# Attention and a two-layer network in one kernel: the first q, k, v transfers in another order and size, and two stores issued at the join

## The chip, the cores and the metric

One Trainium2 chip, one of its cores. The metric is the device time of one execution in microseconds (us), smaller is better; runs of one kernel are given by their median. The profiled execution is a further one, with a time of its own.

## The reference

Softmax attention over 8 batches, 12 heads, 448 positions and 64 columns per head, then a two-layer network over the 3584 tokens, without biases and with a leaky ReLU between the layers:

```python
scores = scale * np.matmul(q, k.transpose(0, 1, 3, 2))
attn = np.exp(scores - np.max(scores, axis=-1, keepdims=True))
attn = attn / (np.sum(attn, axis=-1, keepdims=True) + 1e-09)
x = np.matmul(attn, v).transpose(0, 2, 1, 3).reshape(3584, 768)
h = x @ w_in                       # 768 x 2048
out = np.maximum(0.01 * h, h) @ w_out   # 2048 x 768
```

All arrays are float32 in DRAM; the kernel computes in bfloat16 with float32 sums.

## The kernel before

**Units.** Attention is cut into 48 units: a unit is two heads of one batch, six units to a batch. For each unit the kernel loads q, k and v (`in_q`, `in_k`, `in_v`), brings them as bf16 into the layouts it needs (`cast`, into `qkb` for q and k, into `v_old`, shown as `x_mix`, for v), turns q and k so that the 64 columns lie on partitions (`transposes`, on TensorE in this part, L301, copied out by VectorE, L305), multiplies q and k (`scores`, L319, four chunks of keys, each into one of three PSUM slots `sc`), takes the exponential on ScalarE (`expo`, L331 and L334), multiplies with v (`pv` and `pairs`, L362, with a column of ones in v that gives the sums), and divides on VectorE (L374, L375). Results `x` are turned into `xT`, on TensorE (L389) or by a DMA transpose on SyncE's queue (L276).

**Network.** Seven blocks of tokens (`cuts`) go through both layers as soon as their units are done; block 0's first layer (L424) is woven between the units of the second batch, later blocks between those that follow. Both layers use sums and differences of blocks of the matrices and of the data (`mix_*`, `deep*`), which saves products. The rest of attention is placed between the second layer's products (`second`, `place`).

**Who does what at the start.** The order of all instructions is written by hand: each engine runs its own in the order in which the program emits them, and waits on semaphores. SyncE's queue loads k and q of unit 0 and k of unit 1 as float32 (`load_one`, L173). GpSimd (POOL) issues all other loads (`load_soft`, L163; `load_w`, L215); these convert to bf16 on the way. Such transfers go through one queue, one behind the other. There are eight semaphores for them, given out in turn: a transfer that gets one again waits until the former one has landed. POOL's issue of a load and POOL's casts share POOL's one instruction stream.

`load_soft(u, n, which)` loads n consecutive units in one transfer per array. `room` gives the tile to load into: at first pieces of tiles that are needed later (`w_in_mix`, `w_mix`, `o`, `deep_mix`, `c`), then tiles of a pool (`fq`, `fk`, `fv`). A tile has room for two units. L219 to L230 issue the loads of the start: q of unit 1; q and then k of units 2 and 3; v of unit 0; v of 1 and 2; q and k of 4 and 5; v of 3 and 4; v of 5; the first piece of w_in (columns 0 to 511).

**The first batch.** `first(u)` runs for u = 0 to 5 and emits: scores of chunks 0 and 1 (and 2, for u below 2) and their exponentials, the transposes of x of unit u - 2, the transposes of q and k of unit u + 1 (eight products), `pv` of unit u - 1 in two halves, and scores and exponentials of the other chunks. The casts of units 0, 1 and 2 and that of v of unit 0 are VectorE's (with ScalarE for unit 0), in `first(0)` and ahead of it; from unit 3, and v of unit 1, on they are POOL's. `supply(u)` emits POOL's part of each step from a list: casts of q and k of a unit (`qk`), of v (`v`), loads, pieces of the weights (`w`).

**Stores.** In the second layer `block_pair(i, c)` computes two row tiles `o1` and `o2` of block i. `late` finishes `o1` with a `join` (VectorE, L698) and appends its store to the list `put`; `put_out` issues what is on the list (`store`, L402, on SyncE's queue). It is called by `late` itself only in the last block; else by `second` after 16 steps of the next pair or at the end, and by `place` after rows of x. SyncE's queue works in order: a DMA transpose or a store that waits holds what is behind it. The tiles `o` come from a pool of three.

Of the kernel before, what the change touches and what calls it, by code (L numbers as in the profile page):

```python
# [10 lines left out]
BF16 = mybir.dt.bfloat16  # L11
# [5 lines left out]
def kernel(  # L17
# [24 lines left out]
    NR = len(cuts) - 1  # L42
# [76 lines left out]
    h = h_pool.tile([P, MD, (KEEP + 1) * P], BF16, name="h")  # L119
# [10 lines left out]
    raw = {}  # L130
# [4 lines left out]
    for t in (w_in_mix, w_mix):  # L135
        t = t.rearrange("p x k n -> p (x k n)")
# [9 lines left out]
    def room(x, new):  # L146

        n = P if x and new else SC
        if not rooms:
            return ld_pool.tile([n, 2, NSC, D], F32, name="f" + "qkv"[x])  # L150
        return rooms.pop(0)[:n].bitcast(F32).rearrange("p (h so d) -> p h so d", h=2, so=NSC)

    def load_soft(u, n, which):
        b, hp = divmod(u, HP)
        hs = slice(2 * hp, 2 * hp + 2 * n)
        for x in which:
            new = x > 0 and u >= HY
            t = room(x, new).rearrange("p h so d -> p (h so d)").bitcast(BF16)
            t = t.rearrange("p (u h so d) -> p u h so d", u=2, h=2, so=NSC)
            for p, so, keys in ((slice(0, D), NSC, slice(0, NSC * D)), (slice(D, P), KC, slice(NSC * D, S))) if new else (  # L160
                (slice(0, SC), NSC, slice(0, S)),
            ):
                nc.gpsimd.dma_start(  # L163
                    out=t[p, :n, :, :so].rearrange("p u h so d -> p (u h) (so d)"),
                    in_=(q, k, v)[x][b, hs, keys].rearrange("h (p so) d -> p h (so d)", so=so),
                )
            for i in range(n):
                raw.setdefault(u + i, {})[x] = t[:, i]

    def load_one(u, x, queue):  # L170
        b, hp = divmod(u, HP)
# [7 lines left out]
    def load(u, parts=(0, 1, 2)):  # L179
        if u < NU and u % 2 == 0:  # L180
            load_soft(u, 2, parts)

    def cast(u, parts=(0, 1, 2), by=nc.gpsimd.tensor_copy):
        if u >= NU:
            return
        for x in parts:
            f = raw[u].pop(x)
            t = qkb[u % NB]
            if x < 2 and (x == 0 or u < HY):
                by(t[:SC, x].rearrange("p so h d -> p h so d"), f)  # L190
            elif x == 1:
                if u < HY + NB:
                    nc.gpsimd.memset(t[:, 1, KC], 0.0)
                by(t[:, 1, :KC].rearrange("p so h d -> p h so d"), f[:, :, :KC])
                by(t[:D, 1, KC, 0], f[:D, 0, KC])
                by(t[D:, 1, KC, 1], f[:D, 1, KC])
            elif u < HY:
                by(v_old[:, u % NV, :, :, :D], f)
            else:
                t = v_sb[u % NV]  # L200
                by(t[:, :2 * KC, :D].rearrange("p (h so) d -> p h so d", h=2), f[:, :, :KC])  # L201
                by(t[:D, 2 * KC, :D], f[:D, 0, KC])
                by(t[D:, 2 * KC + 1, :D], f[:D, 1, KC])
# [7 lines left out]
    def load_w(n=1):  # L211
        for _ in range(n):
            if w_steps:
                o, i = w_steps.pop(0)
                nc.gpsimd.dma_start(out=o, in_=i)  # L215
# [3 lines left out]
    load_one(1, 1, nc.sync)  # L219
    ident = const_pool.tile([P, P], BF16)  # L220
    make_identity(nc, ident)
    load_soft(1, 1, (0,))
    load_soft(2, 2, (0, 1))
    load_soft(0, 1, (2,))
    load_soft(1, 2, (2,))
    load_soft(4, 2, (0, 1))
    load_soft(3, 2, (2,))
    load_soft(5, 1, (2,))
    load_w(1)

    warm = h_mix.rearrange("p m c t -> p (m c t)")[:, :512]
    nc.vector.memset(warm, 0.0)
# [160 lines left out]
    def store(o, t0, cols=slice(0, DM), queues=(nc.sync, nc.sync)):  # L393

        queues = list(queues)
        done = 0
        while done < P:
            b, j = divmod(t0 + done, S)
            so, p = divmod(j, SC)
            n = min(SC - p, P - done)  # L400
            dst = out[b * S:(b + 1) * S].rearrange("(p so) n -> so p n", so=NSC)
            queues.pop(0).dma_start(out=dst[so, p:p + n, cols], in_=o[done:done + n, cols])  # L402
            done += n
# [104 lines left out]
    def token(i, x):  # L508

        return KEEP * P if x == KEEP else cuts[i] + x * P  # L510
# [98 lines left out]
    kept, parts, put = {}, [], []  # L609

    def put_out():

        while put:
            store(*put.pop())
# [50 lines left out]
    def block_pair(i, c):  # L665
# [17 lines left out]
        def product(ps, x, w, first=False, cols=slice(0, NW)):  # L683
            for m in range(MH):
                if m in (2, 4, 6):
                    yield
                nc.tensor.matmul(  # L687
                    ps[:, cols], x[:, m], w[:, m], start=(first and m == 0), stop=(m == MH - 1), skip_group_check=True,
                )

        def keep(o, at, ps, by=nc.vector.tensor_copy):
            by(o[:, at], ps[:, :NW])  # L692
# [4 lines left out]
        def join(o, at, ps):  # L697
            nc.vector.tensor_add(o[:, at], o[:, at], ps[:, :NW])  # L698
# [22 lines left out]
        def late():  # L721
            yield from product(b, s3, t3)
            if i:
                keep(o2, left, b, calm)
            join(o2, right, b)
            if i + 1 == NR:
                store(o2, t0, right)
            yield
            yield from product(a, h[:, hi, one], w_out_sb[:, hi, right])
            join(o1, right, a)  # L730
            put.append((o1, token(i, x1)))
            if i + 1 == NR:
                put_out()

        def closing():
# [42 lines left out]
        for x, _ in enumerate(late()):  # L778
            if i and not c and (x == 4 or x == 6 and i + 1 == NR):
                next(parts[0])  # L780
            yield
# [75 lines left out]

    def supply(u):

        for what, n, *parts in {0: [('qk', 3), ('v', 1), ('v', 2), ('load', 6)], 1: [('qk', 4), ('v', 3), ('load', 8, (0, 1))], 2: [('qk', 5), ('v', 4), ('w', 1)], 3: [('qk', 6), ('v', 5), ('w', 1)], 4: [('qk', 7), ('v', 6), ('load', 10, (0, 1)), ('load', 8, (2,))], 5: [('qk', 8), ('v', 7), ('load', 10, (2,)), ('load', 12)]}[u]:  # L860
            if what == "qk":
                cast(n, (0, 1))
            elif what == "v":
                cast(n, (2,))
            elif what == "load":
                load(n, *parts)
            else:
                load_w(n)

    def first(u):  # L870
# [23 lines left out]
        if u + 1 < HP:  # L894
            supply(u)
# [4 lines left out]
        if u + 1 == HP:  # L900
            supply(u)
# [354 lines left out]
```

## Time and profile before

| | |
|---|---|
| time, median of 3 runs | 378.96 us (378.73 to 379.22) |
| profiled execution: time | 379.29 us |
| profiled execution: span of the instructions | 377.5 us |
| granted TensorE clock, mean | 0.995 of full speed |
| VectorE, ScalarE, GpSimd busy | 255.2, 259.8, 193.6 us |
| DMA: bytes moved | 48.08 MB, 127 GB/s over the span, 189 in the first 30 us |
| TensorE busy in the first 30 us | 26.3 us |
| TensorE busy from 30 to 110 us | 79.9 us |

How to read it: times count from the start of the span. PE is TensorE, DVE VectorE, ACT ScalarE, POOL GpSimd; SPq is SyncE's queue of DMA issues. A row of a group or time line names the engine, the line of the kernel, the operation, the tile written and the tile read, and how many instructions were merged (x6). In square brackets stands the idle time of the engine just before, and what ended it; that is inferred, and where the engine named had long been done it was another, mostly a DMA. Granted clock is TensorE's, as a share of full speed.

### The profile page before, as it was taken

To read this page: it belongs to the slowest core of one execution; us is meant where nothing else is said; L and a number is where in the kernel's file an instruction comes from. 1 tells how busy PE (TensorE), PEld (TensorE's weight loads), DVE (VectorE), ACT (ScalarE), POOL (GpSimd) and SP (SyncE) were. 2 spreads that over 40 slices of the span, in tenths; PEclk is the share of its full clock that TensorE was granted. 3 is DMA by queue.
4 is the path that set the end of the run, shared out by engine and by line. 5 is a ranking of instruction groups with operands and counts; after the bars stand their busy time and mean duration, and the time that the engine had idled before them with its cause. 6 is when DMAs were issued, how large, how long until landed. Compare 5 with 4: busy or idle time off the path is not lost.

```text
span 377.5 us, 10113 instructions
## 1 busy us (share of the span) xinstructions
PE 370.0 (98%) x4008; PEld 265.7 (70%) x4008; DVE 255.2 (68%) x558; ACT 259.8 (69%) x399; POOL 193.6 (51%) x376
## 2 busy tenths in 40 slices
PE   7999999999999999999999999999999999999996
PEld 3665657755698556996569966599665995679765
DVE  5666758778666867666687675775747775675763
ACT  6897885866768876658766587666787668526721
POOL 8985972985168889624388234792338020000000
PEclk9899999999999999999999999999999999999999
DMA  9999999998499977974869748889445740131123
GB/s 160 200 204 206 194 198 201 143 153 170 72 185 103 170 119 120 202 159 62 130 139 143 157 64 79 175 136 178 63 65 108 132 109 0 38 98 42 44 63 106
DMA packets 99600, 48.08 MB, mean 127 GB/s; under 512 B 64608, under 2 KB 96352, under 8 KB 99552
## 3 DMA queue, kind: packets, MB, share of 16 engines
q0 software_dynamic: 39600, 22.47, 44.8%
q1 hardware_dynamic: 59504, 24.50, 33.0%
q8 instruction: 31, 0.51, 0.6%
q10 hardware_dynamic: 448, 0.47, 0.4%
q14 instruction: 17, 0.14, 0.1%
HBM read 45.61 MB, written 11.01 MB: 150 GB/s over the span
## 4 chain that ended last, share of the span: by engine, by line
PE 94%; DMA 2%; DVE 1%; issue 1%; ACT 1%; SPq 0%; POOL 0%; DVEq 0%; POOLq 0%; ACTq 0%
PE g L687 29%; PE g L548 14%; PE sc L548 14%; PE sc L322 7%; PE sc L350 6%; PE sc L319 4%; PE g L424 4%; PE sc L650 4%; PE sc L362 3%; PE g L824 2%; PE sc L343 2%; PE g L362 1%; PE g L301 1%; DMA w_in_mix<-in_q_dram 1%; DMA out_dram<-o 1%; PE sc L424 1%
## 5 line engine op out<-in xcount | busy, mean ns | idle before, releaser
L331 ACT ACTIVATE e<-sc 128x896 bf16<-128x896 f32 (+1 forms) x144 | 123.6, 922 | 30.6 <-PE sc L322 20.5
L687 PE MATMUL g<-w_out_sb,h 128*128 128x384 bf16 (+1 forms) x440 | 84.1, 325 | 0.2 <-DVE o L692 0.2
L687 PEld LDWEIGHTS <-h 128*128 128x128 bf16 x592 | 54.4, 98 | 41.8 <-issue 11.7
L537 ACT ACTIVATE h<-c 128x512 bf16<-128x512 f32 (+1 forms) x72 | 43.1, 610 | 30.2 <-DVE c L563 12.4
L548 PEld LDWEIGHTS <-w_in_sb 128*128 128x128 bf16 x576 | 54.6, 98 | 5.7
L190 POOL COPY qkb<-fq 112x512 bf16<-112x512 bf16 x34 | 25.2, 741 | 46.0 <-DMA qkT<-qkb 37.0
L548 PEld LDWEIGHTS <-w_in_mix 128*128 128x128 bf16 x432 | 40.5, 98 | 3.7
L201 POOL COPY v<-fv 128x384 bf16<-128x384 bf16 x30 | 18.6, 618 | 41.5 <-PE sc L350 36.3
L692 DVE COPY o<-g 128x384 f32<-128x384 f32 x47 | 25.9, 552 | 14.7 <-PE g L687 11.4
L350 PE MATMUL sc<-v,e 128*128 128x65 bf16 x720 | 33.3, 193 | 0.0
L981 DVE RECIPROCAL rec<-sc 112x8 f32<-112x8 f32 x42 | 8.7, 207 | 35.8 <-PE sc L350 16.6
L322 PE MATMUL sc<-qkT 64*128 64x448 bf16 (+1 forms) x210 | 32.8, 352 | 0.0
L350 PEld LDWEIGHTS <-e 128*128 128x128 bf16 x720 | 31.2, 98 | 1.3
L982 DVE TENSOR_TENSOR x<-sc,rec 112x512 bf16<-112x512 f32 x42 | 29.0, 691 | 1.6 <-DVE rec L981 0.2
L548 PE MATMUL g<-xT,w_in_sb 128*128 128x256 bf16 (+1 forms) x216 | 28.5, 268 | 0.0
L548 PE MATMUL sc<-xT,w_in_sb 128*128 128x256 bf16 (+1 forms) x216 | 28.5, 268 | 0.0
L698 DVE TENSOR_TENSOR o<-o,g 128x384 f32<-128x384 f32 x39 | 21.3, 549 | 8.7 <-PE g L687 3.9
L343 PE MATMUL sc<-v,e 128*128 128x130 bf16 x120 | 26.5, 221 | 0.0
L654 DVE TENSOR_TENSOR o<-o,sc 128x192 f32<-128x192 f32 x39 | 13.7, 351 | 18.3 <-PE sc L650 18.3
L687 PE MATMUL g<-w_mix,h 128*128 128x384 bf16 x128 | 24.6, 326 | 0.0
L163 POOL DMA_DIRECT2D fv<-in_v_dram x32 | 20.2, 648 | 4.9 <-DMA fq<-in_q_dram 1.5
L362 PEld LDWEIGHTS <-e 112*128 112x128 bf16 x432 | 20.8, 100 | 2.1 <-issue 0.8
(149 smaller groups left out, 744.4 us busy)
## 6 DMA issues: line engine op xcount, KB each, us to landing
fq<-in_q_dram POOLq DMA_DIRECT2D x17, 224.0 KB, 6.1
w_out_sb<-in_moe_w_out_dram POOLq DMA_DIRECT2D x4, 768.0 KB, 12.6
out_dram<-o SPq DMA_DIRECT2D x7, 336.0 KB, 3.4
w_in_sb<-in_moe_w_in_dram POOLq DMA_DIRECT2D x2, 1152.0 KB, 12.6
out_dram<-o SPq DMA_DIRECT2D x7, 288.0 KB, 3.9
fk<-in_k_dram POOLq DMA_DIRECT2D x15, 128.0 KB, 6.1
fv<-in_v_dram POOLq DMA_DIRECT2D x15, 128.0 KB, 5.3
out_dram<-o SPq DMA_DIRECT2D x7, 240.0 KB, 3.3
```

The lines of the kernel that those rows point to most:

```text
L190: by(t[:SC, x].rearrange("p so h d -> p h so d"), f)
L322: nc.tensor.matmul(ps[:, j, :S].rearrange("p (so s) -> p so s", so=NSC), t[p, 1, c], t[p, 0, :, :SC], start=True, stop=True,)
L331: nc.scalar.activation(e[:, :, c, :], ps[:n, :, :S], AX.Exp, scale=scale)
L343: nc.tensor.matmul(ps, e[:, EM + qc * SC:EM + qc * SC + P], vt[:, 2 * KC:].rearrange("p j d -> p (j d)"), start=True, stop=False, skip_gro ...
L350: nc.tensor.matmul(ps[:, j * (D + 1):(j + 1) * (D + 1)], e[:, at:at + P], vt[:, j * KC + c], start=False, stop=(c == KC - 1), skip_group_c ...
L362: nc.tensor.matmul(ps[:, qc, :], t[:SC, at:at + P], vt[:, c], start=(c == 0), stop=(c == NSC - 1),)
L537: nc.scalar.activation(hs[:, m:m + 2, cols], x.rearrange("p (m t) -> p m t", m=2), AX.Prelu, alpha=0.01)
L548: nc.tensor.matmul(ps[:, j * nh:(j + 1) * nh], w[:, kk, ts(j, P)], x[:, kk], start=(first and j == 0 and kk == 0), stop=(kk == KH - 1), sk ...
L687: nc.tensor.matmul(ps[:, cols], x[:, m], w[:, m], start=(first and m == 0), stop=(m == MH - 1), skip_group_check=True,)
L692: by(o[:, at], ps[:, :NW])
L698: nc.vector.tensor_add(o[:, at], o[:, at], ps[:, :NW])
L982: nc.vector.tensor_mul(x, ps[:, :, :, :D], rec.to_broadcast([SC, 2, 2 * NP, D]))
```

## The change

Three things are changed.

1. The loads at the start. `load_soft` can be given a tile and a place in it, so that two transfers share a tile. q and k of units 2 and 3, one transfer each before, become four transfers of one unit, and the order becomes: q of 1, q of 2, k of 2, v of 0, q of 3, k of 3, then v of 1 and 2 and the rest as before. q of 1 and 2 share a tile, as do k of 2 and 3. POOL issues two loads more; bytes and sizes of the packets are the same.
2. The first piece of w_in is no longer issued at the end of the start's loads, but in `supply(0)`: behind POOL's casts of q and k of unit 3 and of v of unit 1, ahead of that of v of unit 2. The list for `supply` changes in this entry alone.
3. `late` calls `put_out` at the join in block 0 and in the last two blocks, where before it did in the last block alone. On SyncE's queue `o1`'s store of the first pair then stands ahead of one DMA transpose of x, once in block 0 and once in block 5; in block 0 two stores at the end of the second pair change places.

The instructions of TensorE, VectorE and ScalarE stay the same, in the same order.

```diff
-    def load_soft(u, n, which):
+    def load_soft(u, n, which, into=None, at=0):
...
-            t = room(x, new).rearrange("p h so d -> p (h so d)").bitcast(BF16)
+            t = (room(x, new) if into is None else into).rearrange("p h so d -> p (h so d)").bitcast(BF16)
...
-                    out=t[p, :n, :, :so].rearrange("p u h so d -> p (u h) (so d)"),
+                    out=t[p, at:at + n, :, :so].rearrange("p u h so d -> p (u h) (so d)"),
...
-                raw.setdefault(u + i, {})[x] = t[:, i]
+                raw.setdefault(u + i, {})[x] = t[:, at + i]
...
-    load_soft(1, 1, (0,))
-    load_soft(2, 2, (0, 1))
+    shared = [room(x, False) for x in (0, 1)]
+    load_soft(1, 1, (0,), shared[0])
+    load_soft(2, 1, (0,), shared[0], 1)
+    load_soft(2, 1, (1,), shared[1])
     load_soft(0, 1, (2,))
+    load_soft(3, 1, (0,))
+    load_soft(3, 1, (1,), shared[1], 1)
     load_soft(1, 2, (2,))
     load_soft(4, 2, (0, 1))
     load_soft(3, 2, (2,))
     load_soft(5, 1, (2,))
-    load_w(1)
...
             put.append((o1, token(i, x1)))
-            if i + 1 == NR:
+            if not 0 < i < NR - 2:
                 put_out()
...
-        for what, n, *parts in {0: [('qk', 3), ('v', 1), ('v', 2), ('load', 6)],
+        for what, n, *parts in {0: [('qk', 3), ('v', 1), ('w', 1), ('v', 2), ('load', 6)],
...
```

More of the change, by code (lines that the diff above doesn't have):

```diff
@@ L858, in supply @@
     def supply(u):
-        for what, n, *parts in {0: [('qk', 3), ('v', 1), ('v', 2), ('load', 6)], 1: [('qk', 4), ('v', 3), ('load', 8, (0, 1))], 2: [('qk', 5), ('v', 4), ('w', 1)], 3: [('qk', 6), ('v', 5), ('w', 1)], 4: [('qk', 7), ('v', 6), ('load', 10, (0, 1)), ('load', 8, (2,))], 5: [('qk', 8), ('v', 7), ('load', 10, (2,)), ('load', 12)]}[u]:
+        for what, n, *parts in {0: [('qk', 3), ('v', 1), ('w', 1), ('v', 2), ('load', 6)], 1: [('qk', 4), ('v', 3), ('load', 8, (0, 1))], 2: [('qk', 5), ('v', 4), ('w', 1)], 3: [('qk', 6), ('v', 5), ('w', 1)], 4: [('qk', 7), ('v', 6), ('load', 10, (0, 1)), ('load', 8, (2,))], 5: [('qk', 8), ('v', 7), ('load', 10, (2,)), ('load', 12)]}[u]:
             if what == "qk":
```

## The prediction

> **What bounds the kernel now.** I read the shares first, then who TensorE (PE) waits for, then the time lines of the stretch in which it waits, engine by engine.
>
> ```profile
> PE 370.0 (98%) x4008; PEld 265.7 (70%) x4008; DVE 255.2 (68%) x558; ACT 259.8 (69%) x399; POOL 193.6 (51%) x376
> ```
>
> PE is busy 370.0 of 377.5 us. An edit that leaves its instructions alone (this one leaves PE's, DVE's and ACT's order as it is) has 7.5 us of idle time and slow clock to work on. Who PE waits for from 23 us to the end:
>
> ```profile
> PE g L687 <- DVE o L692: 0.2, 1, 0.2
> PE sc L319 <- ACT e L331: 0.2, 1, 0.2
> ```
>
> So behind 23 us PE waits 0.4 us in all; what else there is lies in the start and behind its last product (374 us). PE, then ACT, there (start, length, engine, line, idle time before and its releaser):
>
> ```profile
> 8.80 1.05 PE L319 MATMUL sc<-qkT 64*128 64x448 bf16 x6 [0.42 <-DVE qkT L305]
> 9.78 0.37 PE L301 MATMUL g<-ident,qkb 112*128 112x112 bf16 x4
> 10.60 0.52 PE L301 MATMUL g<-ident,qkb 112*128 112x112 bf16 x4 [0.45 <-DVE qkb L190]
> ```
>
> ```profile
> 9.30 2.55 ACT L331 ACTIVATE e<-sc 112x896 bf16<-112x896 f32 x3
> 12.52 0.92 ACT L334 ACTIVATE c<-sc 112x896 bf16<-112x896 f32 x1 [0.67 <-PE sc L319]
> 14.00 2.53 ACT L331 ACTIVATE e<-sc 112x896 bf16<-112x896 f32 x3 [0.56 <-PE sc L319]
> ```
>
> Unit 2's eight transposes are cut in half: the four of q run, the four of k wait 0.45 us for VectorE's cast. Behind them stand P·V of unit 0, the last scores of unit 1 and the first of unit 2, and ACT's exponentials of those start 0.67 + 0.56 = 1.23 us late. After 14.00 ACT shows no idle time until 27.2, and PE is paced by it until 23.05; from there PE runs through. What ACT gains before 14.00 the end gains. Why the cast is late, DVE and then POOL:
>
> ```profile
> 7.02 0.29 DVE L190 COPY qkb<-w_in_mix 112x512 bf16<-112x512 bf16 x1 [1.39 <-DMA w_in_mix<-in_q_dram]
> 8.66 0.65 DVE L190 COPY qkb<-w_in_mix 112x512 bf16<-112x512 bf16 x1
> 9.32 1.22 DVE L190 COPY qkb<-w_in_mix 112x512 bf16<-112x512 bf16 x1
> 10.46 0.28 DVE L198 COPY x_mix<-w_in_mix 112x512 bf16<-112x512 bf16 x1
> ```
>
> ```profile
> 8.38 0.85 POOL L215 DMA_DIRECT2D w_in_sb<-in_moe_w_in_dram  x1 [0.42 <-PE sc L319]
> 9.21 1.17 POOL L190 COPY qkb<-w_in_mix 112x512 bf16<-112x512 bf16 x2
> 11.06 1.17 POOL L198 COPY x_mix<-w_in_mix 112x512 bf16<-112x512 bf16 x2 [0.68 <-DMA w_in_mix<-in_v_dram]
> ```
>
> One copy takes 0.29 us at 7.02, 0.65 us under w_in's issue, and 1.22 us under POOL's two casts of unit 3: it ends 0.16 us behind them (10.54 against 10.38), so it stood still meanwhile. POOL's casts kept their 0.62 us each. Both the late landing of k (below) and this collision come from units 2 and 3 sharing a transfer.
>
> Lastly the granted clock, by 3.4 us windows (PE's busy time is the second number, the clock stands behind POOL's):
>
> ```profile
> 3.85:7.26 3.41, 2.63 (x27) 1.37 (x25) 1.02 (x5) 2.21 (x5) 3.35 (x5) 1.00 1.19 180
> 7.26:10.67 3.41, 2.30 (x22) 1.11 (x23) 2.94 (x6) 3.41 (x5) 2.68 (x4) 1.00 1.42 191
> 10.68:14.08 3.40, 3.40 (x42) 2.29 (x42) 1.83 (x6) 2.17 (x4) 3.02 (x5) 0.50 1.44 196
> ```
>
> PE was busy 2.30 us in the second window, and the third ran at half clock; behind 2.63 us it did not.
>
> **The change, part by part.**
>
> *Transfers.* DMA issues, with KB and us to landing:
>
> ```profile
> w_in_mix<-in_k_dram POOLq DMA_DIRECT2D x1, 224.0 KB, 6.3
> w_in_mix<-in_v_dram POOLq DMA_DIRECT2D x1, 224.0 KB, 6.6
> w_in_mix<-in_q_dram POOLq DMA_DIRECT2D x1, 112.0 KB, 5.5
> w_in_mix<-in_v_dram POOLq DMA_DIRECT2D x1, 112.0 KB, 6.2
> ```
>
> With POOL's issue times these landed thus: q of unit 1 at 1.53 + 5.5 = 7.0; k of 2 and 3 at 3.0 + 6.3 = 9.3; v of 0 at 3.7 + 6.2 = 9.9; v of 1 and 2 at 4.4 + 6.6 = 11.0. POOL's next instruction after q of 2 and 3 waited for their landing: 8.38. From 7.0 to 11.0 these are 784 KB in 4.0 us, about 0.58 us for each 112 KB, and the small v transfer took the same 0.58 as half a large one: splitting costs the queue nothing that shows. So after the change, by bytes ahead in the queue (estimates): q2 7.7, k2 8.4, v0 8.9, q3 9.3, k3 9.9, v of 1 and 2 as before.
>
> *VectorE.* Its copy of unit 1's transposes still ends at 8.74. Then q2, k2 and v0 are all there and POOL has no cast to run before q3's landing at 9.3: three copies of 0.29 us end near 9.6. Upper bound: each meets POOL as at 9.32, and v0 ends at 10.7 as now. I take the free row, since POOL's cast is the only thing that has shown the long one and comes after them.
>
> *PE.* No cut in the transposes: eight from 9.78 in 0.41 us (the later groups of eight are followed 0.41 us on), P·V of unit 0 starts at 10.2 instead of 10.91. It then lasts 0.5 us (the pace of P·V at 14.41) instead of 1.0. With the half clock still granted from 10.68: scores of chunk 3 end at 11.2, the second half of P·V at 12.2, unit 2's first scores at 12.75; the exponential at 14.00 starts at 12.8, a gain of 1.2. With full clock all that is ready by 11.9, and ACT's own chain sets 14.00 − 1.23 = 12.77. Either way about **1.2 us**; bounds 0 (upper bound above) and 1.4 (ACT's lengths overlap by up to 0.1 us an instruction).
>
> By the clock rows the second window gains 0.45 us of transposes and P·V, 2.75 us or more, above the 2.63 that kept the clock. The Trainium skill, "TensorE: Matmul & The Clock Gate", Part 1, has these 4096-cycle windows free-running, not reset when a kernel starts; the 3.41 us agree with the trace. By that rule the same idle time may fall into other windows in other executions, which would move the sum between 1.0 and 1.4; no run here shows another phase.
>
> *POOL.* Two more issues of 0.70 us. Its order: v5's issue to 9.2, casts q3 and k3 to 10.5 (k3 lands at 9.9), v1's cast at 11.06 as now, then w_in's issue to 12.5, v2's cast to 13.1, unit 6's three issues to 15.2. So POOL is 0.9 us later than before. Who waits behind it: unit 4's casts (end 16.3; PE wants them at 18.63 − 1.2 = 17.4), v2 (13.1 against 16.3), unit 5 (19.4 against 20.6). It catches up at 21.84, where it stood waiting for a landing anyway. Cost 0; without this cover 0.9.
>
> *w_in.* Issued at 11.7 instead of 8.38. The queue in front of it holds the same bytes: in the packet records the data of v5 end at 14.2 and w_in's follow at once, although it was issued 5.7 us before; an issue takes some 2.2 us to its first packet (1.53 to 3.70). 11.7 + 2.2 = 13.9: no gap, at worst 0.3 us. PE uses w_in at 25.89, its data end at 17.8. Cost 0.
>
> *Stores.* The diff also puts blocks 0 and 5's stores at the join:
>
> ```profile
> 333.14 0.56 DVE L692 COPY o<-g 128x384 f32<-128x384 f32 x1 [1.17 <-DMA out_dram<-o]
> 329.63 1.04 SPq L402 DMA_DIRECT2D out_dram<-o  x2
> ```
>
> DVE waits 1.17 us for a buffer whose store was queued on SP behind a transpose that had to wait until 328.4; its join was done at 324.6. Stored there it lands some 4 us sooner, and PE's 0.21 us at 333.75 go. On SP two issues of 0.5 us now stand ahead of that transpose, which has 3 us of room, and in block 0 ahead of one at 88.49, which may slip 0.5 us; PE waits for neither. Gain **0.2**, bounds 0 and 0.2.
>
> *Sum.* 1.2 + 0.2 = 1.4: span 377.5 → 376.1. The profiled execution took 379.29, 0.33 above the median of 378.96; from the median, 377.6.
>
> **Rivals.** About 0.2% (0.76 us) is what a measurement of this kernel can tell from no change: "faster" is below 378.2.
>
> B, *the collision moves on to v0.* k2 is early, but v5's issue delays q2 as w_in's did (0.65), q3's cast gets in at 9.3, and VectorE's k2 or v0 stands until k3's cast ends near 10.5. P·V starts at 10.7: gain 0.2, with the stores 378.5. For: DVE at 9.32 did not get in between two casts. Against: k3 lands only at 9.9, which leaves gaps. The Trainium skill, "SBUF — State Buffer", "Who interferes with whom", says the same as a rule: a VectorE copy in a two-port mode and a GpSimd instruction lock each other out for a whole instruction, and the first to start wins. By that rule B decides at 9.3; the 1.22 us agree with it.
>
> C, *VectorE loses to POOL's whole row of casts (slower).* Place: the same port, one copy earlier. If v5's issue holds q2 to 9.3 and q3's cast starts ahead of k2, k2 stands to 10.5 and ends at 10.8; v0 then ends at 11.1 only if it starts before v1's cast at 11.06, or else behind it (0.6 us) near 11.95. P·V of unit 0 then starts at 12.0 instead of 10.91: 378.96 + 1.1 − 0.2 = 379.8. It decides at the end of q2's copy: later than 9.3, or q3 landed before it. For: w_in's issue did hold q2 by 0.36 us at 8.66. Against: the 0.29 us copy at 7.02 met v5's and v3's issues and was not held, and k3's landing leaves POOL a gap.
>
> D, *it runs into landings that do not move.* The queue is saturated to 85 us, so a PE that is 1.2 us earlier meets data at their old times. The closest is unit 6's k: cast at 22.4, wanted at 24.98 − 1.2 = 23.8. If 1.3 us of lateness on the queue ate that, only the stores' gain is left: 378.75.
>
> E, *the clock gate closes one window later.* PE, early, waits for ACT's buffers between 10.68 and 14.09; if it is busy there for less than some 2.3 to 2.6 us, 14.09 to 17.5 runs at half clock. That window holds 3.2 us of PE work at full clock and loses 1.6: 378.96 − 1.4 + 1.6 = 379.2. Against: I count about 3.0 us of work there.
>
> **How the numbers follow.** Forecast 0.62 (377.2 to 378.1: from 1.4 early with 0.2 of spread between runs, to 0.65 early where one of the three copies is held for a cast), B 0.18, D 0.07, C 0.06, E 0.04, something not seen 0.03. Faster: the forecast and mild forms of B and D, 0.67. Slower: C and what is not seen, 0.09. Same: the rest, 0.24. The range reaches from ACT's full overlap with some 0.3 of spread between runs, 376.9, over B and D to 378.9.
>
> **What would show it.** Right: PE's 0.45 us before L301 near 10.6 gone, three VectorE copies of about 0.3 us before 9.7, ACT's third group of exponentials at 12.8, no DVE wait for out at 333. Wrong: a copy of 1 us on VectorE at 9.3 to 10.5 (B), the k2 copy itself late (C), clock 0.50 behind 14.1 (E), or PE's early gain gone again between 17 and 60 us (D).

## The result and the profile after

| | before | after |
|---|---|---|
| time, median of 22 runs each, on the same chip | 378.70 us (377.88 to 379.22) | 379.62 us (378.28 to 381.49) |
| after over before, 95% interval | | 1.0027 (1.0015 to 1.0039) |
| profiled execution: time and span | 379.29, 377.5 us | 381.49, 379.7 us |
| granted clock, mean | 0.995 | 0.999 |

After is slower by 0.9 us, where 1.4 us of gain were forecast. Its profiled execution is the slowest of its 22: its stalls are read for their place, and prices come from the medians.

The early part went as forecast. Time lines of after, VectorE, then TensorE, then ScalarE (start, length, engine, line, operation; the diff moves all lines behind L222 on by three):

```profile
8.69 0.49 DVE L190 COPY qkb<-w_in_mix 112x512 bf16<-112x512 bf16 x2
9.09 0.41 DVE L198 COPY x_mix<-w_in_mix 112x512 bf16<-112x512 bf16 x1
```

```profile
10.62 0.57 PE L304 MATMUL g<-ident,qkb 112*128 112x112 bf16 x8
```

```profile
6.93 2.53 ACT L334 ACTIVATE e<-sc 112x896 bf16<-112x896 f32 x3 [1.19 <-PE sc L322]
9.34 0.93 ACT L337 ACTIVATE c<-sc 112x896 bf16<-112x896 f32 x1
10.14 2.55 ACT L334 ACTIVATE e<-sc 112x896 bf16<-112x896 f32 x3
12.53 0.97 ACT L337 ACTIVATE c<-sc 112x896 bf16<-112x896 f32 x1
13.32 2.59 ACT L334 ACTIVATE e<-sc 112x896 bf16<-112x896 f32 x3
```

The three copies end at 9.50, the eight transposes of unit 2 run uncut, and ScalarE has no idle time from 6.93 to 26.57. Its third group starts 6.39 us behind its first; in the profile of before it was 7.91 us. Yet it starts at 13.32, not at 12.8, for the first group is 0.8 us later than before: 0.68 us are left of the gain in this profile (14.00 to 13.32). The windows of 3.4 us (TensorE's busy time second, granted clock behind the five busy times, last GB/s of all transfers) show no half clock in after:

```profile
7.26:10.67 3.41, 2.22 (x20) 0.93 (x19) 1.77 (x6) 3.41 (x5) 3.20 (x5) 1.00 1.30 167
10.68:14.08 3.40, 3.15 (x67) 2.49 (x66) 2.03 (x6) 3.40 (x5) 2.50 (x5) 1.00 1.40 186
14.09:17.50 3.41, 3.20 (x60) 2.19 (x57) 2.30 (x8) 3.41 (x6) 3.41 (x7) 1.00 1.17 171
```

The last number is the first sign of trouble: 171 GB/s from 14.09 to 17.50, where before moved 208. TensorE's waits in after (us in total, times, longest) name what is new behind 23 us:

```profile
PE sc L322 <- DMA qkT<-qkb: 1.4, 1, 1.4
...
PE g L690 <- DVE o L701: 0.6, 1, 0.6
PE sc L322 <- DVE x L985: 0.5, 1, 0.5
```

**The queue.** POOL's time line in after:

```profile
9.53 1.16 POOL L190 COPY qkb<-w_in_mix 112x512 bf16<-112x512 bf16 x2 [0.15 <-ACT e L334]
11.59 0.61 POOL L198 COPY x_mix<-w_in_mix 112x512 bf16<-112x512 bf16 x1 [0.90 <-DMA w_in_mix<-in_v_dram]
12.14 0.85 POOL L215 DMA_DIRECT2D w_in_sb<-in_moe_w_in_dram  x1
```

The issue of w_in stands behind v of unit 1's cast, which waited for its landing until 11.59. So it starts at 12.14. The first packet of w_in follows at 14.64, 2.5 us after the start of the issue; the data of v of unit 5, ahead of it, had ended at 14.55. From 14 to 24 us the DMA view gives GB/s in 40 slices of 0.25 us, before and then after:

```profile
GB/s 193 223 205 215 197 262 193 205 197 209 193 201 205 201 207 188 197 197 186 197 197 199 197 191 195 199 199 195 193 197 197 199 195 191 201 195 197 213 201 215
DMA packets 3146, 2.01 MB, mean 201 GB/s; under 512 B 101, under 2 KB 3145, under 8 KB 3145
```

```profile
GB/s 174 217 117 129 139 164 180 180 180 184 168 184 197 180 188 180 176 193 166 172 176 119 135 156 162 180 178 164 180 174 186 197 197 199 191 197 193 197 201 195
DMA packets 2731, 1.76 MB, mean 176 GB/s; under 512 B 89, under 2 KB 2730, under 8 KB 2730
```

After drops to 117 GB/s at 14.5 and again to 119 at 19.25, and only from 21.5 on it stays above 185. In ten us it moves 1.76 MB instead of 2.01; at 201 GB/s that is 1.2 us of transfers lost. The ends of the data in the queue, from counting the bytes of its packets:

```
us, end of data         before   after   later by
v of unit 5              14.01   14.55    0.54
w_in, first piece        17.91   19.14    1.23
q, k, v of 6 and 7       21.43   23.07    1.64
w_in, last piece         35.17   36.84    1.67
w_out, first piece       48.14   51.35    3.21
q, k of 14 and 15        63.49   66.96    3.47
```

The step to 3.2 us is POOL's: its first issue of w_out stands behind a cast that waits for a landing, and moves from 41.12 to 43.33. POOL in after:

```profile
41.89 1.50 POOL L198 COPY x_mix<-o 112x512 bf16<-112x512 bf16 x2 [0.45 <-DMA o<-in_v_dram]
43.33 0.75 POOL L215 DMA_DIRECT2D w_out_sb<-in_moe_w_out_dram  x1
```

**Where TensorE pays.** At 41 us. VectorE's time line of before, then of after:

```profile
36.44 0.56 DVE L473 TENSOR_TENSOR w_in_mix<-w_in_sb 128x768 bf16<-128x768 bf16 x1 [1.89 <-DMA w_in_sb<-in_moe_w_in_dram]
```

```profile
38.33 0.56 DVE L476 TENSOR_TENSOR w_in_mix<-w_in_sb 128x768 bf16<-128x768 bf16 x1 [3.29 <-DMA w_in_sb<-in_moe_w_in_dram]
38.92 1.15 DVE L476 TENSOR_TENSOR w_in_mix<-w_in_sb,w_in_mix 128x768 bf16<-128x768 bf16 x2
39.99 0.20 DVE L984 RECIPROCAL rec<-sc 112x8 f32<-112x8 f32 x1
40.23 0.69 DVE L985 TENSOR_TENSOR x<-sc,rec 112x512 bf16<-112x512 f32 x1
```

The sums over w_in's last piece start 1.9 us later; the division of a unit stands behind them in VectorE's order and frees the PSUM slot of the next scores only at 40.92. TensorE, after:

```profile
39.90 0.55 PE L322 MATMUL sc<-qkT 64*128 64x448 bf16 x4
40.97 0.36 PE L322 MATMUL sc<-qkT 64*128 64x448 bf16 x2 [0.52 <-DVE x L985]
```

The next unit's scores follow at 44.50, 4.60 us behind 39.90; before had 3.91 (40.54 to 44.45). In this profile that costs 0.69, which uses up the 0.68 us of lead. At 73 us, TensorE and POOL of after:

```profile
73.59 0.55 PE L322 MATMUL sc<-qkT 64*128 64x448 bf16 x4
75.54 0.36 PE L322 MATMUL sc<-qkT 64*128 64x448 bf16 x2 [1.39 <-DMA qkT<-qkb]
```

```profile
67.47 0.88 POOL L190 COPY qkb<-fq 112x512 bf16<-112x512 bf16 x1 [8.87 <-DMA fq<-in_q_dram]
```

Unit 14's cast (63.52 before) and with it its turning by DMA are 4 us late, and the last two products wait. What follows is 1.62 us later than before (the second layer's products resume at 75.83 against 74.21). The third wait, 0.56 at 88.47, isn't the change's alone: a further profile of before shows 0.56 at 85.73. So the 0.68 us that were left of the early gain were spent at 41 us, and the wait at 75 us made after slower.

### The profile page after: what moved, and what is told of

Same layout as the page of the kernel before. It is cut to its first block, busy times and chain, and to the rows that moved or that the text cites. A ratio compares the mean times of both kernels' runs of the same rounds, so it can differ in the third digit from the quotient of the medians.

```text
span 379.7 us, 10119 instructions
## 1 busy us (share of the span) xinstructions
PE 370.2 (97%) x4008; PEld 265.9 (70%) x4008; DVE 257.2 (68%) x558; ACT 259.8 (68%) x399; POOL 192.0 (51%) x378
## 4 chain that ended last, share of the span: by engine, by line
PE 91%; ACT 3%; DMA 2%; DVE 1%; issue 1%; POOL 0%; ACTq 0%; DVEq 0%; POOLq 0%
PE g L690 29%; PE g L551 14%; PE sc L551 14%; PE sc L325 7%; PE sc L353 6%; PE g L427 4%; PE sc L653 4%; PE sc L322 3%; PE sc L365 3%; ACT e L334 3%; PE sc L346 2%; DMA qkT<-qkb 2%; PE g L827 1%; PE g L304 1%; DMA w_in_mix<-in_k_dram 1%; PE g L365 1%
## 5 line engine op out<-in xcount | busy, mean ns | idle before, releaser
L690 PEld LDWEIGHTS <-h 128*128 128x128 bf16 x592 | 54.4, 98 | 41.8 <-issue 11.7
L190 POOL COPY qkb<-fq 112x512 bf16<-112x512 bf16 x34 | 23.9, 704 | 46.7 <-DMA qkT<-qkb 36.8
L322 PE MATMUL sc<-qkT 64*128 64x448 bf16 x144 | 20.1, 355 | 3.7 <-DMA qkT<-qkb 1.4
```

The costliest lines, as they stand in the source:

```text
L322: nc.tensor.matmul(ps[:, j, :S], t[p, S + c * SC:S + c * SC + P], t[p, :S], start=True, stop=True)
L690: nc.tensor.matmul(ps[:, cols], x[:, m], w[:, m], start=(first and m == 0), stop=(m == MH - 1), skip_group_check=True,)
```

## The experiments

Three things were open: what each part is worth by itself; whether the early gain is real; and how a w_in that TensorE first needs at 25.9 us can cost anything. All kernels compute the whole of the reference.

**The parts alone.** e1_stores is before with only the stores moved:

```diff
-            if i + 1 == NR:
+            if not 0 < i < NR - 2:
```

> Only the stores at the join (blocks 0 and 5). Theory Q (the changed kernel is slower because its load queue runs later: its data from w_in on come 1.2 to 3.4 us later in the profile, and TensorE stands 1.39 us at 75.5 us for unit 14's turned q and k): the stores have no part in it, 0 to 0.2 us faster than before, ratio 0.9995 to 1.0. Rival S (the stores put ahead of the transposes on SyncE's queue cost the time): 0.7 to 1 us slower, ratio 1.002 or more.

Measured: 378.54 us, ratio 0.9987 (0.9976 to 0.9999). Ratios, here and below, are to before on the same chip, as recorded; they aren't the quotients of the medians (378.54 over 378.69 is 0.9996). VectorE no longer waits for a store at the copy that stood at 333.14 before:

```profile
331.76 0.56 DVE L692 COPY o<-g 128x384 f32<-128x384 f32 x1 [0.31 <-PE g L687]
```

The stores are worth about what was forecast (0.2 us is 0.9995, inside the interval). TensorE's wait that hung on it, 0.20 to 0.27 us near 333, stands in all six profiles with the stores at their old place and in none of the ten with the new one. The same profile has the old transfers, and shows something else, on VectorE and on ScalarE:

```profile
9.07 1.88 DVE L190 COPY qkb<-w_in_mix 112x512 bf16<-112x512 bf16 x2
10.88 0.28 DVE L198 COPY x_mix<-w_in_mix 112x512 bf16<-112x512 bf16 x1
```

```profile
10.25 2.56 ACT L331 ACTIVATE e<-sc 112x896 bf16<-112x896 f32 x3
12.64 0.97 ACT L334 ACTIVATE c<-sc 112x896 bf16<-112x896 f32 x1
13.44 2.60 ACT L331 ACTIVATE e<-sc 112x896 bf16<-112x896 f32 x3
```

VectorE's copies collide with POOL's casts as in the first profile (1.88 us for two), and ScalarE has no gap all the same. In this execution the clock went to full at 7.13 us and stayed there; in the profile of before it did so at 3.85 and fell back from 10.68 to 14.09.

e2_win is before with only w_in moved (the `load_w(1)` at the start's end goes, `('w', 1)` enters `supply(0)` behind `('v', 1)`).

> Only w_in's first piece issued later (behind the casts of unit 3 and of v of unit 1); transfers and stores as before. Theory Q with the gap at w_in as its cause: the queue runs dry near 14 us, the data behind it come 0.5 us or more later than before, and the late data are met near 74 us: as slow as the changed kernel or up to 0.5 us faster, ratio 1.000 to 1.003; VectorE's copies of unit 2 lose the 0.36 us under w_in's issue, but still meet POOL's casts. Rival P (the split transfers slow the queue): data as before, time as before or faster, ratio 0.998 to 1.000.

Measured: 379.66 us, 1.0030 (1.0011 to 1.0049). Issue at 12.47, first piece 4.87 us of data instead of 3.90. TensorE has both of after's waits, at 41.27 and 75.32 us:

```profile
PE sc L318 <- DMA qkT<-qkb: 0.9, 1, 0.9
PE sc L318 <- DVE x L981: 0.6, 1, 0.6
```

This part alone gives the whole slowdown.

e3_split is after with w_in's issue and the stores as before: only the transfers are split.

```diff
+    load_w(1)
...
-            if not 0 < i < NR - 2:
+            if i + 1 == NR:
...
-        for what, n, *parts in {0: [('qk', 3), ('v', 1), ('w', 1), ('v', 2), ('load', 6)],
+        for what, n, *parts in {0: [('qk', 3), ('v', 1), ('v', 2), ('load', 6)],
...
```

> Only the split and reordered transfers; w_in's first piece is issued at the end of the start's loads as before, stores as before. Theory Q with the gap at w_in as its cause: no gap, the data from w_in on as before, the early gain of 0.7 to 1.2 us is kept: ratio 0.997 to 0.999. Rival P (the split transfers slow the queue): the data come 1 us or more late, ratio 1.001 to 1.003.

Measured: 378.56 us, 0.9996 (0.9981 to 1.0012). No wait for DMA behind 23 us, the queue on time (3.90 us for w_in's first piece). The expected gain isn't there: 1.2 us would be 0.9968, outside the interval.

e4_split_win is the split with w_in moved, the stores as before (after with only the line of the stores put back).

> The split transfers and the late w_in together, without the stores. Theory Q and rival P: as the changed kernel, ratio 1.002 to 1.004. Rival S (stores): as before or faster, ratio up to 1.000.

Measured: 380.03 us, 1.0029 (1.0015 to 1.0044), 1.47 us above e3_split on the same chip. Its profile was its fastest run (378.71) and has 0.2 us of the first stall and nothing of the second. So w_in's new place costs 1.0 us without the split (e2_win) and 1.5 us with it; the intervals don't tell the two apart. The parts add up: by the ratios −0.0004 (split), −0.0013 (stores) and +0.0033 (w_in's place, e4 over e3) make 1.0016, inside the interval of after's 1.0027 (1.0015 to 1.0039).

x3_split_stores is split and stores, with w_in at its old place.

> The changed kernel without the move of w_in: split transfers and stores alone. Theory Q: the two small effects add, ratio to before 0.9975 to 0.9995, no wait on DMA, w_in's data end near 18.3. Rival: the stores need the late queue or harm with the split, ratio 1.000 or more.

Measured: 378.30 us, 0.9981 (0.9961 to 1.0001): the change without its third part is a little faster or the same.

**Is the early gain real?** Before was run twice more for a profile of its own.

> The kernel before once more, for another profile. Theory H (the 1.23 us of ScalarE's idle time from which the forecast took its gain belong to one position of the clock's windows): where no window at half clock lies between 8 and 14 us, the third group of exponentials starts 6.4 us behind the first one, as in the kernels that were tried so far (7.9 in the first profile). Rival: 7.9 us in this profile too.

> As the profile above, a third one of the kernel before: 6.4 us from the first to the third group of exponentials if no half-clock window lies there, near 7.9 if one does.

Measured: 378.29 and 379.22 us, spans 376.5 and 377.4. In both ScalarE's third group starts 6.40 and 6.39 us behind the first, with the old transfers. The clock by profile, with that distance:

```
profile            clock full from    falls back       first to third group, us
before                  3.85          10.68 to 14.09          7.91
x6_mid_again (split)    3.98          10.80 to 14.22          7.13
b1, b2 (before)         5.15, 5.85    no                      6.40, 6.39
e3 (split)              5.17          no                      6.40
e1 (before's loads)     7.13          no                      6.40
after                   6.65          no                      6.39
```

Of all 16 profiles two have the half clock there, the two in which the clock rose earliest (the next is 4.86). Only these two have a gap of 0.5 us or more in ScalarE's row between the first and third group; in the others the distance is 6.39 or 6.40 us, but 6.66 in e2_win. x6_mid_again (below) is such a case with the split in place; its windows and ScalarE's row:

```profile
7.26:10.67 3.41, 2.10 (x24) 1.02 (x23) 1.43 (x4) 3.41 (x6) 3.41 (x6) 1.00 1.33 168
10.68:14.08 3.40, 3.40 (x44) 2.11 (x42) 1.84 (x5) 2.84 (x5) 3.40 (x6) 0.52 1.37 181
```

```profile
12.31 0.92 ACT L337 ACTIVATE c<-sc 112x896 bf16<-112x896 f32 x1
13.79 2.53 ACT L334 ACTIVATE e<-sc 112x896 bf16<-112x896 f32 x3 [0.56 <-PE sc L322]
```

The 0.67 us of idle time are gone, the 0.56 are not, and the clock falls back all the same. TensorE was busy 2.10 us in the window ahead (2.30 in before's). Busy time in one window doesn't decide it: 2.24 us at 6.57 to 9.98 in x5, 2.29 at 5.94 to 9.36 in e2 and 2.29 at 7.08 to 10.49 in x2 kept the clock. The Trainium skill, "TensorE: Matmul & The Clock Gate", Part 1, has the windows free-running, with the step at a place that varies between runs; that it lies anywhere from 3.85 to 7.13 us here, counted from the span's start, agrees, but it is more than the 500 ns either way that the page gives.

The mean granted clock is recorded for each execution of the experiments, without a place in the span. Of before's 115, 98 have 0.998 or more, with a median of 378.68 us. Twelve have 0.994 or 0.995, as before's profile has (one window of 3.41 us at half clock makes 0.995), and their median is 379.94. Five have 0.990 or 0.991, with 381.48. So one such window goes with about 1.3 us, the size of the gain that was forecast, but in one execution of ten, and a median doesn't show it. A mean of 0.996 or less stands in 22 of 151 executions with the old transfers (before, e1, e2, x5), and in 5 of 130 with the split. So the split seems to make the half clock rarer; no experiment was made for that alone, and e3, the split by itself, has 0 of 12.

**How late may w_in be?** x1_win_mid issues it behind unit 3's two casts, ahead of the cast that waits for v of unit 1; x2_win_later a cast further behind than after.

```diff
-        for what, n, *parts in {0: [('qk', 3), ('v', 1), ('w', 1), ('v', 2), ('load', 6)],
+        for what, n, *parts in {0: [('qk', 3), ('w', 1), ('v', 1), ('v', 2), ('load', 6)],
...
```

```diff
-        for what, n, *parts in {0: [('qk', 3), ('v', 1), ('w', 1), ('v', 2), ('load', 6)],
+        for what, n, *parts in {0: [('qk', 3), ('v', 1), ('v', 2), ('w', 1), ('load', 6)],
...
```

> The changed kernel with w_in's first piece issued one POOL cast earlier, directly behind the casts of unit 3: issue near 10.7 instead of 12.1 us. Theory Q (the queue runs dry because the issue comes later than 2.2 to 2.5 us ahead of the end of the data before it, near 14.2 us): no gap or a small one, w_in's data end near 18.3 as in the kernel without the move, no wait on DMA at 75 us: ratio to before 0.997 to 0.9995. Rival M (what costs is that w_in stands behind casts at all, or in supply's place): as the changed kernel, 1.002 to 1.004.

> The changed kernel with w_in's first piece issued one POOL cast later, behind that of v of unit 2: issue near 12.7 us instead of 12.1. Theory Q: the gap grows by about 0.6 us, w_in's data end near 19.6, and the waits at 41 and 75 us grow with it: ratio to before 1.003 to 1.006. Rival N (it is not how late the issue is): as the changed kernel, 1.0015 to 1.004.

Measured: x1 378.17 us, 0.9973 (0.9955 to 0.9991); x2 379.57 us, 1.0015 (0.9997 to 1.0033). x1's w_in came on time (0.3 us of wait at 40.40 are left). x2, though later still, is not slower than after, against what was expected. A second measurement of x1:

> The version with split, stores and w_in behind unit 3's casts once more, beside the one without the split on the same chip. Theory Q: issue near 10.2 us, no late data, ratio to before 0.997 to 0.999, faster beyond the interval.

378.59 us, 0.9990 (0.9971 to 1.0010): in the range, but not beyond the interval as expected. And x5_nosplit, x1 with before's unsplit transfers:

> The two other parts without the split: q and k of units 2 and 3 in one transfer each, w_in's first piece directly behind POOL's casts of unit 3, stores at the join. Theory H: the split by itself does nothing for the time where the clock is full, so this is as the kernel with the split (0.9973): 0.997 to 0.999. Rival (the split's early casts are worth something): 0.9985 to 1.000, 0.3 us or more behind the version with the split.

378.39 us, 0.9995 (0.9973 to 1.0016), whose ratio lies in the rival's range, while its median is 0.2 us below x6's and not 0.3 above: undecided. The kernels by the start of w_in's issue (lengths and ends from counts of the bytes):

```
              issue   data of w_in's    end of data,    unit 14's last     ratio
                      first piece, us   q, k of 14/15   scores start
before         8.38       3.90             63.49           73.54           
x3             9.01       3.87             63.84           72.81           0.9981
e3             9.24       3.90             63.97           72.42           0.9996
x5             9.64       3.94             63.42           72.69           0.9995
x1 / x6       10.2        3.90 / 3.95      64.82 / 63.72   73.03 / 74.10   0.9973 / 0.9990
e4            11.57       4.37             64.96           72.99           1.0029
after again   11.88       4.96             66.94           74.72           1.0020
after         12.14       4.59             66.96           75.54           1.0027
e2            12.47       4.87             67.07           75.32           1.0030
x4            12.91       4.98             67.11           75.67           1.0041
x2            13.43       5.06             66.72           74.67           1.0015
```

(Where unit 14's scores are cut in two, the second part's start stands; before and x6 are the two profiles with the half clock.) There is a step, not a slope: up to 10.2 us the piece takes 3.9 us; from 11.6 on it takes 4.4 to 5.1. From the issue to the end of the data ahead (v of unit 5) it is 4.1 us or more in the first group and 1.7 to 2.6 us in the second; where between 2.6 and 4.1 the step lies, no run shows. Behind it the lateness doesn't grow with the issue's: unit 14's q and k end at 66.7 to 67.1 in all of the second group but e4's fastest run. That is why x2 isn't slower. It has one long wait at 42 us,

```profile
PE sc L322 <- DVE x L985: 1.6, 1, 1.6
```

and comes to unit 14 so late that q and k are there. The waits at 41 and 75 us are two ways to pay for one lateness.

**Move the sums.** x4_mix_later is after with VectorE's sums over w_in spread otherwise, none behind the unit that stalled at 41 us:

```diff
-                for _ in range({5: 3, 6: 3, 7: 2, 8: 1, 9: 2, 10: 1}.get(m, 0)):
+                for _ in range({5: 3, 7: 3, 8: 3, 9: 2, 10: 1}.get(m, 0)):
```

> The changed kernel with VectorE's sums over w_in's last piece placed two steps of the first layer later, so that they no longer stand ahead of unit 6's division while that piece is late. If the 0.7 us that TensorE loses near 41 us come from VectorE waiting there for w_in's last piece (0.5 us of it shown as a wait on x), that stall goes: 0.3 to 0.7 us faster than the changed kernel, ratio to before 1.000 to 1.002; the wait at 75 us stays. If not: as the changed kernel, 1.002 to 1.004.

Measured: 380.29 us, 1.0041 (1.0015 to 1.0066); a miss. The stall at 41 us is gone (scores at 39.80 and 43.71), and another stands two units later, where five sums now lie in a row ahead of a division:

```profile
49.38 0.37 PE L322 MATMUL sc<-qkT 64*128 64x448 bf16 x2 [1.21 <-DVE x L985]
```

The wait at unit 14 stays (0.93). Moving the consumers doesn't help; the queue has to be mended.

**The queue or w_in itself?** Two theories were left. Q: the time that the queue loses when the next transfer comes too late makes everything behind it late. W: w_in's own late arrival does it. y1_load6_first keeps w_in behind v of unit 1's cast, but issues q, k and v of units 6 and 7 at the end of the start's loads, so that the queue is full meanwhile and w_in's first piece itself comes last. After was measured again beside it.

```diff
     load_soft(5, 1, (2,))
+    load(6)
...
-        for what, n, *parts in {0: [('qk', 3), ('v', 1), ('w', 1), ('v', 2), ('load', 6)],
+        for what, n, *parts in {0: [('qk', 3), ('v', 1), ('w', 1), ('v', 2)],
...
```

> The changed kernel once more, beside the next one. Both theories: ratio to before 1.0015 to 1.004, the queue's data 0.5 to 1.7 us late from w_in on, waits near 41 and 75 us.

> The changed kernel with unit 6's three loads issued at the end of the start's loads, ahead of POOL's casts of unit 3; w_in's first piece stays behind the cast of v of unit 1 and is issued near 13 us. Theory Q (the queue's lost time is what costs): no gap, since the queue has 672 KB, 3.5 us, to move meanwhile; w_in's first piece ends near 21.7 us, 2.5 us later than in the changed kernel, but what follows comes as in the kernel before; no wait on DMA at 75 us: ratio to before 0.997 to 0.9995. Rival W (w_in's own lateness costs): slower than the changed kernel, 1.003 to 1.006.

Measured: after again 379.61 us, 1.0020 (1.0008 to 1.0033); y1 378.19 us, 0.9971 (0.9955 to 0.9987). Their difference is 1.4 us. After again has the queue's lateness (23.31 for units 6 and 7) but not the two waits that were expected: like x2 it has one of 1.4 us at 42.09, none at 75, and a further one on POOL's cast of unit 6's k:

```profile
24.78 0.37 PE L304 MATMUL g<-ident,qkb 112*128 112x112 bf16 x4 [0.42 <-POOL qkb L190]
```

POOL's time line and the DMA view of 14 to 24 us in y1:

```profile
10.44 0.71 POOL L163 DMA_DIRECT2D w_mix<-in_v_dram  x1
11.13 1.18 POOL L190 COPY qkb<-w_in_mix 112x512 bf16<-112x512 bf16 x2
12.24 0.62 POOL L198 COPY x_mix<-w_in_mix 112x512 bf16<-112x512 bf16 x1
12.79 0.84 POOL L215 DMA_DIRECT2D w_in_sb<-in_moe_w_in_dram  x1
```

```profile
GB/s 195 199 197 197 193 188 195 246 186 184 180 193 195 199 205 205 211 205 199 221 197 205 213 209 205 217 197 209 201 193 199 203 195 191 195 203 190 199 215 262
DMA packets 3148, 2.02 MB, mean 202 GB/s; under 512 B 103, under 2 KB 3146, under 8 KB 3146
```

w_in is issued 0.65 us later than in after, and its first piece ends last of these loads, at 21.57 instead of 19.14. Yet there is no hole, the piece takes 3.82 us, the sum of these loads ends at 21.57 (21.43 before, 23.07 after), and TensorE waits neither at 41 nor at 75 us (unit 14's scores run uncut at 72.94). W falls; what costs is the queue's lost time. y1 and x1_win_mid beat both kernels; the second measurement of x1 shows that so small a lead isn't certain. Part of it is before's half clock: without the executions of 0.996 or less the medians make 0.9985 for both.

## Why the prediction was wrong

*w_in, "Cost 0".* This is the step that failed. The prediction put its issue at 11.7 and its first packet at 13.9, against v of unit 5's end at 14.2. Measured were 12.14, 14.64 and 14.55. Two terms slid: the cast ahead of the issue waits for v of unit 1's landing and started at 11.59 instead of 11.06, and issue to first packet took 2.5 instead of 2.2 us. The first lies within the spread between executions: over the 16 profiles that transfer landed at 10.66 to 12.30 us with the split and at 10.68 to 11.86 without. A margin of 0.3 us was less than that. "At worst 0.3 us" took a late transfer to cost its own gap alone. The gap was 0.1 us, but the first piece then took 4.59 us instead of 3.90, and the loads of units 6 and 7 behind it 3.93 instead of 3.52.

*The lateness behind it.* The prediction asked only when TensorE needs w_in (25.89). It had rival D's places, 17 to 60 us, with too early a TensorE in place of a late queue. Unit 6's k, which it called the closest, cost 0.42 us in the second profile of after and 0.24 in x4's, but the large waits came elsewhere. Nor is the queue saturated to 85 us, as D has it: in the profile of before DMA moves 26 GB/s from 71 to 73 us. VectorE already stood waiting 1.89 us for w_in's last piece in the profile of before, and POOL 8.04 us for unit 14's q. Those were waits on the queue with no slack at all, and in after both pass its lateness on to TensorE.

*The early gain, 1.2 us.* This is the second step that failed. In after the local signs came out: three copies by 9.5, the 0.45 us wait gone. But the late cast alone doesn't make the gap in ScalarE's row: it needs the half clock of 10.68 to 14.09, which lies there in 2 of 16 profiles. The prediction noted that the windows may fall elsewhere and put that at 0.2 us; it takes nearly the whole gain away. Split alone: 0.9996 (0.9981 to 1.0012). In the one profile of the split with the half clock, x6, the distance of the groups shrank by 0.78 us, not 1.2, and the second window held 2.10 us of work, not the 2.75 that was counted on. What may be left of the argument is the rarer half clock, 5 of 130 executions against 22 of 151.

*POOL, "cost 0", and the collision.* VectorE was free of POOL as forecast, in after and in e3. Unit 4's and 5's casts cost TensorE nothing. POOL's lateness counted through w_in's issue, and at unit 6's k in two of the late profiles.

*Stores, 0.2 us.* Right in size, 0.9987 (0.9976 to 0.9999), and in mechanism: VectorE's and TensorE's waits near 333 us are gone.

*Rivals and range.* B, C and E didn't come, and D came from the other side. The slower case that was needed lay in the paragraph on w_in itself, carried on through 41 and 75 us; without it 379.62 fell outside the range.

**What stays open.** Why w_in's piece is slower throughout when it is issued late, and why the queue dips a second time at 19.25, although the transfer that follows there was issued 5.6 us earlier, as far ahead as before. All six late profiles show the slower pace for units 6 and 7 too (3.9 to 4.0 us; 3.5 to 3.7 where w_in was on time). In e4 the issue comes 2.64 us ahead of the end of the data before it, more than the 2.2 us that the prediction took for the way to the first packet, and the piece is slow all the same. What sets the half clock: the busy time of the window ahead alone doesn't. And the wait of 0.56 us near 86 to 88, which some profiles of before, after, e2 and y1 have and others don't.

## What to carry to other kernels

In a deep queue, count a moved issue's slack from the landing that the issuing engine itself waits for, plus the time from issue to first packet, and treat a margin of less than one such time as none (here 2.6 us from the issue to the end of the data ahead weren't enough, and 4.1 were). Ask for everything behind it in the queue, not for the moved transfer alone, and look for engines that already stand waiting for the queue. A stall that sits under a stretch of half clock should be looked for in several executions before its removal is counted as a gain.

## What the runs showed that was not expected

- A transfer that reaches a queue just as it runs out doesn't only start late: 768 KB took 4.4 to 5.1 us where 3.9 is usual, with 117 GB/s at first and mostly 164 to 197 behind.
- The clock rises to full between 3.85 and 7.13 us of the span (16 profiles; the kernel before alone: 3.85, 5.15 and 5.85). In the two where it rose by 4 us it fell back from 10.7 to 14.1 or 14.2, and the gaps near 10 us reached ScalarE's row.
- VectorE's collision with POOL's casts (two copies in 1.88 us instead of 0.49) cost nothing in e1: at full clock ScalarE, which ran without a gap there, and not TensorE, set the pace.
